# Where the split second weights and the split hidden values of a two-layer expert kernel lie in on-chip memory

## The chip, the cores and the metric

One core of a Trainium2 chip. The metric is the device time of one execution in microseconds (us); the lower, the better.

## The reference

A transform, then two mixture-of-experts layers on the same 24,576 tokens of 256 numbers:

```python
X = np.fft.fft(x, axis=1); X = np.fft.fft(X, axis=2); x = X.real      # 8 x 3072 x 256
# each layer (the first normalises its router's operands and divides by tau):
expert_idx = np.argmax(logits, axis=1); gate_w = softmax(logits)[expert_idx]
for e in range(8):
    h = np.maximum(x[mask] @ w1[e], 0.0)                             # 256 -> 1024
    out[mask] = gate_w[mask, None] * (h @ w2[e])                     # 1024 -> 256
```

The inputs and outputs are float32. The second layer takes the output of the first as its input, and routes anew.

## The kernel before

The transform is done by matmuls with tables of cosines and sines. Its tokens are scattered by indirect DMAs into a table in device memory that is sorted by expert. After that the work runs in blocks ("slots") of one expert each: in layer one 41 blocks of 512 tokens and 17 half blocks of 256, in layer two the same again. Four more half blocks of each layer stand in conditionals and are not executed with these inputs. A block loads its rows, and its expert's weights if the expert has changed, then does two products.

Every operand of these products is split into a high and a low part (`float32r`, 4 bytes a number), and each product is done as three matmuls: high by high, low by high, high by low.

- First product, `mm1` (line 1169): per block 48 matmuls (lines 1183 to 1185) of 512 columns (a half block: 48 of 256). The first weights w1h and w1l are the stationary operand, the tokens xh and xl (tile `a`) the moving one. `evac_h` (line 1187) turns the result into the tiles hh (by ACT, with relu) and hl (by the vector engine, DVE): eight rows, f = 0 to 7, of 512 numbers per partition.
- Second product, `mm2` (line 1196): for each of the four groups of 128 tokens (two in a half block), and for each f, three matmuls: hh by w2h (line 1202), hl by w2h (1203), hh by w2l (1204). Here hh and hl are the stationary operand, 128 columns at a time, and row f of w2h or w2l is the moving one. In layer two a row has 256 numbers. In layer one it has 264: eight columns more give the next layer's router logits.
- `split2` (line 1123) makes w2h (ACT) and w2l (DVE) for the next block while a block computes. Both tiles have two buffers, used in turn; hh and hl have one each.

The order of all this is written out by a planner (class `Plan`) with due times; the second weights' split falls beside the products of the block before. In the built program the engines' queues hold it in that order.

Where a tile's rows lie is set by hand. Lines 1127 to 1130 give the row width w, the offset o of w2h in its tile, and the further offset z of w2l, all in numbers of 4 bytes; lines 1172 to 1175 give the width of the rows of hh and hl and their offset, 16. Before, a row of layer one is as wide as its data, 264, and begins at 32 + 264 f (w2h) or 40 + 264 f (w2l), so its address is a multiple of 64 bytes or 32 bytes past one in turn; hh and hl have rows of 520. In layer two rows are 256 wide from offset 0, and those of hh and hl 512 wide from offset 16. In the built program the tiles' own starts are multiples of 64 bytes, and modulo 256 bytes they are all the same.

The identity matrix `ident` (line 240) is made by two POOL instructions (`make_identity`, line 243) and read by the transposes of `gate_columns` (line 980) during the transform.

Of the kernel before, what the change touches and what calls it, by code (L numbers as in the profile page):

```python
# [10 lines left out]
F32 = mybir.dt.float32  # L11
F32R = mybir.dt.float32r
# [207 lines left out]
def build(tc, x, x0, prep, ctab, ctab8, t2, t2t, misc, embt, tau, w1a, w2a, w2t, wg2, w1b, w2b, out):  # L220
    nc = tc.nc
# [4 lines left out]
    with ExitStack() as top:  # L226
        cp = top.enter_context(tc.tile_pool(name="const", bufs=1))
# [6 lines left out]
            name=nc.get_next_instruction_name(), act_func_set_id=EXP_LN_SET, ins=[], outs=[], engine=A.engine))  # L234
# [2 lines left out]

        mt = cp.tile([128, _o], F32, name="mt")
        mc = {k: mt[:, a:b] for k, (a, b) in MISC.items()}
        ident = cp.tile([128, 128], F32, name="ident")  # L240
        ones = cp.tile([128, 128], BF16, name="ones")
        V.memset(ones, 1.0)
        make_identity(nc, ident)
        tri = cp.tile([128, 128], BF16, name="tri")
        carry = [cp.tile([128, 8], F32, name=f"carry{i}") for i in range(2)]
        rw1 = cp.tile([128, 2, F], F32, name="rw1")
# [255 lines left out]
        fp = fx.enter_context(tc.tile_pool(name="fft", bufs=1))  # L502
# [9 lines left out]
        tb1 = fp.tile([128, 1], F32, name="tau1")  # L512
        wg = fp.tile([128, 2, 32], F32, name="wg")
        V.memset(wg, 0.0)
        onef = fp.tile([128, 128], F32, name="onef")
        V.memset(onef, 1.0)
        tiny = fo.tile([128, 1], F32, name="tiny", bufs=1)
# [538 lines left out]
        slots = []  # L1056
# [9 lines left out]
        pools = {}  # L1066
# [56 lines left out]
        def split2(i, q):  # L1123
            st = S_[i]
            raw = st["raw"]
            if "w2h" not in st:
                w, o, z = (264, 32, 8) if slots[i][0] == 0 else (256, 0, 0)
                for n, k in (("w2h", o), ("w2l", o + z)):
                    t = pools["sb"].tile([128, 8 * 264 + 64], F32R, name=n)
                    st[n] = t[:, k : k + 8 * w].rearrange("p (a b) -> p a b", a=8)  # L1130
            fs = slice(2 * q, 2 * q + 2)
            pairs = [(raw[1][:, fs], fs, slice(0, 256))]
            if slots[i][0] == 0 and q == 0:
                pairs.append((raw[2].rearrange("p (a b) -> p a b", b=8), slice(0, 8), slice(256, 264)))
            for src, f, cs in pairs:
                hi = st["w2h"][:, f, cs]
                act(hi, src, AF.Copy)
                tt(V, st["w2l"][:, f, cs], src, hi.bitcast(F32), ALU.subtract)
# [30 lines left out]
        def mm1(i, k):  # L1169
            st, n, nf = S_[i], 128 * slots[i][3], 4 // slots[i][3]  # L1170
            if k == 0:
                w = 520 if slots[i][0] == 0 else 512
                for e, gap in (("hh", 128), ("hl", 80)):
                    t = pools["sb"].tile([128, 8 * 512 + gap], F32R, name=e, bufs=1)
                    st[e] = t[:, 16 : 16 + 8 * w].rearrange("p (a b) -> p a b", a=8)
            ps = st["ph", k] = pools["h"].tile([128, 512], F32, name="ph")
            for g in range(nf):
                f = nf * k + g
                fs = slice(f * 128, f * 128 + 128)
                o = ps[:, g * n : g * n + n]  # L1180
                for c in range(2):
                    a, z = (g == 0 and c == 0), (g == nf - 1 and c == 1)
                    P.matmul(o, st["w1h"][:, c, fs], st["xh"][:, c, :n], start=a, stop=False)  # L1183
                    P.matmul(o, st["w1h"][:, c, fs], st["xl"][:, c, :n], start=False, stop=False)  # L1184
                    P.matmul(o, st["w1l"][:, c, fs], st["xh"][:, c, :n], start=False, stop=z)  # L1185
# [64 lines left out]
        def stages(plan, i, t):  # L1250

            layer, key, j, ns = slots[i]
            a, tB = dA[i], t[1]
            for k in range(2 * ns):
                plan.add(t[0] + a * k / (2 * ns), lambda i=i, k=k: mm1(i, k))
                plan.add(t[0] + a * (k + 1) / (2 * ns) + 0.1, lambda i=i, k=k: evac_h(i, k))
            for q in range(ns):
                plan.add(tB + 2.75 * q, lambda i=i, q=q: mm2(i, q))
                plan.add(tB + 2.75 * (q + 1) + 0.1, lambda i=i, q=q: evac_y(i, q))
            te = tB + 2.75 * ns + 0.5  # L1260
            plan.add(tB + 0.2, lambda i=i: ids(i))
            if layer == 0:
                st = S_[i]
                route(plan, te, ns, lambda st=st, ns=ns: st["gt"][:, :ns],
                      lambda st=st, ns=ns: [(st["y"][:, :ns, 256:257], 0, ns)], 1, lambda q, st=st: st["y"][:, q, 0:W],
                      lambda: qr.tile([128, 512], F32, name="pr"), dt=0.3, rank=3.6 if i in (0, 1, 4, 5) else 1.8,
                      pen=(lambda st=st: st["pen"]) if ns == 2 else None)
                plan.add(te + 2.5, lambda i=i: put_ids(i))
                plan.add(te + 1.3, lambda i=i: split_y(i))
            else:  # L1270
                for q in range(ns):
                    plan.add(te + 0.1 * q, lambda i=i, q=q: store(i, q))
            return te
# [4 lines left out]
        def rest(layer):  # L1278
# [4 lines left out]
            def block(j):  # L1283
                i = n_ + layer * (NS - NSF) + j - NSF
                if not own:
                    R = [fo.tile([128, 8, W], F32, name="R", bufs=6).rearrange("p a b -> p (a b)") for _ in range(3)]
                    own["x"] = pools["sb"].tile([128, 4, 256], F32, name="xk", bufs=1).rearrange("p a b -> p (a b)")[:, 0 : 2 * W].rearrange("p (a b) -> p a b", a=2)
                    for k, n in enumerate(("xh", "xl")):
                        o = 2 * W + k * 512
                        own[n] = R[0][:, o : o + 512].bitcast(F32R).rearrange("p (a b) -> p a b", a=2)  # L1290
                    own["raw"] = (
                        R[1][:, 0 : 2 * F].rearrange("p (a b) -> p a b", a=2),
                        R[2][:, 0 : 8 * D].rearrange("p (a b) -> p a b", a=8),
                        R[0][:, 2 * W + 1024 : 2 * W + 1088],
                    )
                S_[i].update(own)
                p = Plan()
                p.add(0.0, lambda: load_rows(i))
                p.add(0.1, lambda: load_w(i, 0))
                p.add(0.2, lambda: load_w(i, 1))  # L1300
                p.add(2.1, lambda: join(i, 0))
                p.add(2.2, lambda: evac_x(i, 0, 0))
                p.add(2.3, lambda: evac_x(i, 0, 1))
                for q in range(4):
                    p.add(3.0 + q, lambda q=q: split1(i, q))
                for q in range(4):
                    p.add(7.0 + q, lambda q=q: split2(i, q))
                stages(p, i, (7.0, 13.0))
                p.run()
                own.update({k: S_[i][k] for k in ("w1h", "w1l", "w2h", "w2l")})  # L1310
# [14 lines left out]
        for i in range(n_):  # L1325
            layer, key, j, ns = slots[i]
            t, a = sA[i], dA[i]
# [7 lines left out]
            for q in range(4):  # L1335
                if q < 2 and i and ns == 4:
                    plan.add(sA[i - 1] + dA[i - 1] + dT[i] + (0.7 + 0.18 * q) * dB[i - 1], lambda i=i, q=q: split2(i, q))
                elif ns == 4:
                    plan.add(t + a * (0.3 + 0.25 * (q - 2)) + 0.3, lambda i=i, q=q: split2(i, q))
                else:  # L1340
                    plan.add(t + a * (-0.08 + 0.21 * q) + 0.3, lambda i=i, q=q: split2(i, q))
# [21 lines left out]
        for k, (b, j) in enumerate([(b, j) for b in range(EARLY, B) for j in (2, 0, 1)]):  # L1363
            t, dt = (sA[1] + 14.0 + 26.0 * k, 2.7) if b <= KNOWN[1] else (sA[n1 + (k - 6) * 2] + 1.0, 5.0)
# [55 lines left out]
```

## Time and profile before

| | us |
|---|---|
| median of 3 runs | 2522.08 (2516.24 to 2531.93) |
| profiled execution, its own time | 2522.99 |
| its span, first to last instruction | 2521.2 |
| TensorE busy | 2464.8 |
| DVE, ACT, POOL busy | 1718.6, 1546.5, 644.0 |

The span is what the trace shows; the 1.8 us around it are not in it. Matmuls overlap each other, so that TensorE's busy time says that it has work, not how fast it goes: for that one takes from the timeline when matmuls start. PE is TensorE's matmuls, PEld its weight loads. Lines are those of the listing.

### The profile page before, as it was taken

To read this page: it belongs to the slowest core of one execution; us is meant where nothing else is said; L and a number is where in the kernel's file an instruction comes from. 1 tells how busy PE (TensorE), PEld (TensorE's weight loads), DVE (VectorE), ACT (ScalarE), POOL (GpSimd) and SP (SyncE) were. 2 spreads that over 40 slices of the span, in tenths; PEclk is the share of its full clock that TensorE was granted. 3 is DMA by queue.
4 is the path that set the end of the run, shared out by engine and by line. 5 is a ranking of instruction groups with operands and counts; after the bars stand their busy time and mean duration, and the time that the engine had idled before them with its cause. 6 is when DMAs were issued, how large, how long until landed. Compare 5 with 4: busy or idle time off the path is not lost. (4 is left out here: it accounts for less than half of the span.)

```text
span 2521.2 us, 47343 instructions
## 1 busy us (share of the span) xinstructions
PE 2464.8 (98%) x16634; PEld 2233.7 (89%) x16634; DVE 1718.6 (68%) x3760; ACT 1546.5 (61%) x3311; POOL 644.0 (26%) x603
## 2 busy tenths in 40 slices
PE   7989999999999999999999999999999999999998
PEld 5767898889988998899898989899999999999998
DVE  7785877766676666666888766555555666555876
ACT  4756676666666666665776655555555555555775
POOL 0486245234342111112111211111111111111111
PEclk9999999999999999999999999999999999999999
DMA  8597555444543354433344322421221344313631
GB/s 302 196 305 226 146 148 152 126 110 135 140 115 81 102 139 117 125 97 73 106 139 106 93 67 66 114 84 44 83 51 49 89 143 116 116 47 128 198 98 33
DMA packets 336054, 302.84 MB, mean 120 GB/s; under 512 B 277454, under 2 KB 294277, under 8 KB 321469
## 3 DMA queue, kind: packets, MB, share of 16 engines
q1 hardware_dynamic: 306600, 223.39, 32.7%
q0 software_dynamic: 28528, 76.20, 9.2%
q8 instruction: 135, 2.21, 0.4%
q14 instruction: 114, 0.93, 0.1%
q10 hardware_dynamic: 677, 0.11, 0.0%
HBM read 292.93 MB, written 91.62 MB: 153 GB/s over the span
## 5 line engine op out<-in xcount | busy, mean ns | idle before, releaser
L1203 PE MATMUL p<-w2h,hl 128*128 128x264 f32 (+1 forms) x3168 | 895.3, 283 | 12.5 <-DVE hl L1193 12.2
L1204 PE MATMUL p<-w2l,hh 128*128 128x264 f32 (+1 forms) x3168 | 890.7, 281 | 0.0
L1202 PE MATMUL p<-w2h,hh 128*128 128x264 f32 (+1 forms) x3168 | 885.7, 280 | 1.1 <-ACT gt L224 1.1
L1193 DVE SCALAR_TENSOR_TENSOR hl<-ph,hh 128x512 fp32r<-128x512 f32 x792 | 544.2, 688 | 285.9 <-ACT hh L224 278.2
L224 ACT ACTIVATE hh<-ph 128x512 fp32r<-128x512 f32 x792 | 470.6, 597 | 362.9 <-PE ph L1185 362.3
L1183 PE MATMUL ph<-a,w1h 128*128 128x512 f32 (+1 forms) x1856 | 669.7, 361 | 4.7 <-DVEq L1312 2.0
L1185 PE MATMUL ph<-a,w1l 128*128 128x512 f32 (+1 forms) x1856 | 666.6, 359 | 0.0
L1184 PE MATMUL ph<-a,w1h 128*128 128x512 f32 (+1 forms) x1856 | 665.9, 359 | 0.4 <-DVE a L223 0.4
L1203 PEld LDWEIGHTS p<-w2h,hl 128*128 128x128 f32 x3168 | 594.7, 188 | 24.7 <-DVE hl L1193 19.3
L1202 PEld LDWEIGHTS p<-w2h,hh 128*128 128x128 f32 x3168 | 596.4, 188 | 5.0 <-ACT gt L224 1.5
L1204 PEld LDWEIGHTS p<-w2l,hh 128*128 128x128 f32 x3168 | 598.2, 189 | 0.0
L223 DVE TENSOR_TENSOR w2l<-rw,w2h 128x512 fp32r<-128x512 f32 x464 | 318.9, 687 | 250.3 <-ACT w2h L224 246.2
L1243 POOL DMA_INDIRECT out<-yo,oix x198 | 194.7, 983 | 890.9 <-ACT yo L224 854.3
L330 POOL DMA_INDIRECT xs<-yo,ix x198 | 214.3, 1082 | 757.9 <-ACT hh L224 489.3
L1183 PEld LDWEIGHTS ph<-a,w1h 128*128 128x128 f32 x1856 | 349.2, 188 | 55.0 <-ACT w2h L224 2.1
L1185 PEld LDWEIGHTS ph<-a,w1l 128*128 128x128 f32 x1856 | 349.3, 188 | 53.6
L1184 PEld LDWEIGHTS ph<-a,w1h 128*128 128x128 f32 x1856 | 349.2, 188 | 50.2 <-DVE a L223 0.7
L223 DVE TENSOR_TENSOR w1l<-rw,w1h 128x512 fp32r<-128x512 f32 x464 | 307.9, 687 | 93.9 <-ACT w1h L224 93.1
L224 ACT ACTIVATE w2h<-rw 128x512 fp32r<-128x512 f32 x464 | 290.7, 627 | 23.0 <-DMA rw<-in_w2b 12.1
L224 ACT ACTIVATE w1h<-rw 128x512 fp32r<-128x512 f32 x464 | 275.2, 626 | 4.0 <-DMA rw<-in_w1a 4.0
L224 ACT ACTIVATE yo<-p,R 128x256 f32<-128x256 f32 x198 | 94.3, 476 | 218.0 <-PE p L1204 216.5
L224 ACT ACTIVATE R<-p,R 128x256 f32<-128x256 f32 x198 | 93.7, 473 | 201.4 <-PE p L1204 201.3
(217 smaller groups left out, 1969.6 us busy)
## 6 DMA issues: line engine op xcount, KB each, us to landing
rw<-in_w1a SPq DMA_DIRECT2D x58, 1024.0 KB
rw<-in_w2a SPq DMA_DIRECT2D x58, 1024.0 KB
rw<-in_w1b SPq DMA_DIRECT2D x58, 1024.0 KB
rw<-in_w2b SPq DMA_DIRECT2D x58, 1024.0 KB
X<-in_x SPq DMA_DIRECT2D x48, 512.0 KB
rw<-in_w2t SPq DMA_DIRECT2D x8, 1024.0 KB
kept<-Rk SPq DMA_DIRECT2D x15, 512.0 KB
xk<-kept SPq DMA_DIRECT2D x12, 512.0 KB
```

The source lines that it names most:

```text
L223: tt = lambda eng, o, a, b, op: eng.tensor_tensor(out=o, in0=a, in1=b, op=op)
L224: act = lambda o, i, f, **k: A.activation(out=o, in_=i, func=f, **k)
L330: table.scattered(G.indirect_dma_start(out=table.buf, out_offset=bass.IndirectOffsetOnAxis(ap=st["ix"][:, j : j + 1], axis=0), in_=rows(j) ...
L1183: P.matmul(o, st["w1h"][:, c, fs], st["xh"][:, c, :n], start=a, stop=False)
L1184: P.matmul(o, st["w1h"][:, c, fs], st["xl"][:, c, :n], start=False, stop=False)
L1185: P.matmul(o, st["w1l"][:, c, fs], st["xh"][:, c, :n], start=False, stop=z)
L1193: V.scalar_tensor_tensor(out=st["hl"][:, fs, :n], in0=ps, scalar=0.0, in1=hi.bitcast(F32), op0=ALU.max, op1=ALU.subtract)
L1202: P.matmul(ps[:, :n], st["hh"][:, f, js], st["w2h"][:, f, :n], start=(f == 0), stop=False)
L1203: P.matmul(ps[:, :n], st["hl"][:, f, js], st["w2h"][:, f, :n], start=False, stop=False)
L1204: P.matmul(ps[:, :n], st["hh"][:, f, js], st["w2l"][:, f, :n], start=False, stop=(f == 7))
L1243: ins = G.indirect_dma_start(out=out, out_offset=bass.IndirectOffsetOnAxis(ap=st["ix"][:, j : j + 1], axis=0), in_=st["y"][:, j, 0:256], i ...
```

## The change

- Layer one: rows of w2h and w2l are 272 numbers (1088 bytes) apart instead of 264. The offset of w2h is 0, 16, 32 or 48 numbers, by the slot's number modulo four; w2l lies 16 further. The columns that are written and multiplied stay 264.
- hh and hl: offset 0 instead of 16; in layer one rows of 528 instead of 520. In layer two they stay 512.
- Layer two: the offset of w2h and w2l is 48 instead of 0.
- The tiles grow by 64 numbers (w2h, w2l) and 48 (hl). To make room, `ident` moves from the pool that lasts through the whole kernel to the one of the transform, whose memory the block tiles take later; with it `make_identity` is recorded one memset of the vector engine later.

The matmuls, their number, shapes and order are the same; every engine's instructions stand in the same order as before. ACT, DVE, SP and POOL each get one wait more, for POOL's two instructions on `ident`, in front of their first use of the memory that `ident` shares.

```diff
-        ident = cp.tile([128, 128], F32, name="ident")
         ones = cp.tile([128, 128], BF16, name="ones")
         V.memset(ones, 1.0)
-        make_identity(nc, ident)
...
         wg = fp.tile([128, 2, 32], F32, name="wg")
         V.memset(wg, 0.0)
+        ident = fp.tile([128, 128], F32, name="ident")
+        make_identity(nc, ident)
...
             if "w2h" not in st:
-                w, o, z = (264, 32, 8) if slots[i][0] == 0 else (256, 0, 0)
+                w, o, z = (272, 16 * (i % 4), 16) if slots[i][0] == 0 else (256, 48, 0)
                 for n, k in (("w2h", o), ("w2l", o + z)):
-                    t = pools["sb"].tile([128, 8 * 264 + 64], F32R, name=n)
+                    t = pools["sb"].tile([128, 8 * 272 + 64], F32R, name=n)
                     st[n] = t[:, k : k + 8 * w].rearrange("p (a b) -> p a b", a=8)
...
             if k == 0:
-                w = 520 if slots[i][0] == 0 else 512
-                for e, gap in (("hh", 128), ("hl", 80)):
-                    t = pools["sb"].tile([128, 8 * 512 + gap], F32R, name=e, bufs=1)
-                    st[e] = t[:, 16 : 16 + 8 * w].rearrange("p (a b) -> p a b", a=8)
+                w = 528 if slots[i][0] == 0 else 512
+                for e in ("hh", "hl"):
+                    t = pools["sb"].tile([128, 8 * 528], F32R, name=e, bufs=1)
+                    st[e] = t[:, 0 : 8 * w].rearrange("p (a b) -> p a b", a=8)
```

## Rows read from the trace of the kernel before

**Rows 1.** The page: span, busy times, and the granted clock in 40 slices.

```profile
PE 2464.8 (98%) x16634; PEld 2233.7 (89%) x16634; DVE 1718.6 (68%) x3760; ACT 1546.5 (61%) x3311; POOL 644.0 (26%) x603
...
PEclk9999999999999999999999999999999999999999
```

**Rows 2.** Waits of TensorE: us in total, times, longest us.

```profile
PE p L1203 <- DVE hl L1193: 12.2, 24, 1.3
```

**Rows 3.** Stretches (us; busy us of each engine, instructions; clock; DMA) by stage.

```profile
251.50:1420.30 1168.80, 1154.02 (x7953) 1053.39 (x7953) 836.38 (x2211) 770.49 (x1562) 320.88 (x293) 1.00 0.46 120
1420.30:2521.20 1100.90, 1091.76 (x7542) 1009.68 (x7540) 697.10 (x1180) 623.14 (x1156) 197.68 (x201) 1.00 0.31 89
```

**Rows 4.** Groups by line and shape (busy us, mean ns, idle): the hh*w2h products.

```profile
L1202 PE MATMUL p<-w2h,hh 128*128 128x264 f32 x1584 | 446.3, 282 | 1.1 <-ACT gt L224 1.1
L1202 PE MATMUL p<-w2h,hh 128*128 128x256 f32 x1584 | 439.4, 277 | 0.0
```

**Rows 5.** Timeline of TensorE (start us, length us): second products of one layer-one block.

```profile
590.98 0.28 PE L1202 MATMUL p<-w2h,hh 128*128 128x264 f32 x1
...
602.53 0.39 PE L1183 MATMUL ph<-a,w1h 128*128 128x512 f32 x1
```

**Rows 6.** Timeline: a layer-two block's second products, its successor's first, and second again.

```profile
1940.52 0.28 PE L1202 MATMUL p<-w2h,hh 128*128 128x256 f32 x1
...
1951.42 0.39 PE L1183 MATMUL ph<-a,w1h 128*128 128x512 f32 x1
...
1962.41 0.28 PE L1202 MATMUL p<-w2h,hh 128*128 128x256 f32 x1
```

**Rows 7.** Timeline: second products of layer one's first block.

```profile
263.96 0.29 PE L1203 MATMUL p<-w2h,hl 128*128 128x264 f32 x1
...
275.60 0.39 PE L1183 MATMUL ph<-a,w1h 128*128 128x512 f32 x1
```

**Rows 8.** Timeline: second products of a slower layer-two block.

```profile
1566.64 0.28 PE L1202 MATMUL p<-w2h,hh 128*128 128x256 f32 x1
...
1577.94 0.40 PE L1183 MATMUL ph<-a,w1h 128*128 128x512 f32 x1
```

**Rows 9.** Timeline: a layer-two half block, 48 first products and then 48 second.

```profile
2323.61 0.28 PE L1183 MATMUL ph<-a,w1h 128*128 128x256 f32 x1
...
2329.05 0.28 PE L1202 MATMUL p<-w2h,hh 128*128 128x256 f32 x1
...
2334.71 0.28 PE L1183 MATMUL ph<-a,w1h 128*128 128x256 f32 x1
```

**Rows 10.** Timeline of POOL: the last instruction on the identity.

```profile
1.04 0.29 POOL masks.py:199 TENSOR_SCALAR_AFFINE_SELECT ident<-ident 128x128 f32<-128x128 f32 x1
```

**Rows 11.** Line 980, the identity's readers: durations min/median/max, first and last start.

```profile
L980 PE MATMUL px<-ident,gs x16: 271/272/273, 54.1 to 217.3; 128*128 128x128 f32 x16
```

**Rows 12.** Groups: ACT's writes of w2h in layer one, then in layer two.

```profile
L224 ACT ACTIVATE w2h<-rw 128x512 fp32r<-128x512 f32 x233 | 146.4, 629 | 12.2 <-DMA rw<-in_w2a 10.8 <-DMA rw<-in_w2b 1.4
...
L224 ACT ACTIVATE w2h<-rw 128x512 fp32r<-128x512 f32 x232 | 144.9, 625 | 12.2 <-DMA rw<-in_w2b 12.1
```

**Rows 13.** Timeline of TensorE: the products of two successive rows in layer one.

```profile
600.01 0.28 PE L1202 MATMUL p<-w2h,hh 128*128 128x264 f32 x1
600.12 0.28 PE L1203 MATMUL p<-w2h,hl 128*128 128x264 f32 x1
600.24 0.28 PE L1204 MATMUL p<-w2l,hh 128*128 128x264 f32 x1
600.37 0.28 PE L1202 MATMUL p<-w2h,hh 128*128 128x264 f32 x1
600.48 0.28 PE L1203 MATMUL p<-w2h,hl 128*128 128x264 f32 x1
600.60 0.28 PE L1204 MATMUL p<-w2l,hh 128*128 128x264 f32 x1
```

**Rows 14.** Timeline of the weight loads: the one beside the first of these.

```profile
600.01 0.19 PEld L1203 LDWEIGHTS p<-w2h,hl 128*128 128x128 f32 x1
```

## The prediction

> **What bounds the kernel now.** I read the page first. TensorE is busy for 2464.8 of 2521.2 us and its granted clock is at the top digit in all 40 slices [rows 1], so this is one long stream of matmuls at 2.4 GHz, the upper level, and a change counts only as far as it changes how fast that stream runs or how often it stops. The waits of TensorE say how often it stops: the largest is 12.2 us over the whole run, L1203 (second half of a product) waiting for the tile hl [rows 2]. The stretches then say where the time lies: layer one takes 1168.8 us from 251.5 on, layer two 1100.9 [rows 3]. The two layers have the same number of matmuls with the second weights, 3 x 1584 each (one of the three products stands in the rows), 264 columns wide in layer one and 256 wide in layer two [rows 4]. These 4752 matmuls of layer one (41 blocks of 96, 17 half blocks of 48) are what the change re-addresses.
>
> A busy time cannot price them, because each matmul lasts about 280 ns while the next starts about 120 ns later. So I take start to start, from the timeline. In a layer-one block the 96 matmuls run from 590.98 to 602.53 us: 11.55 / 96 = 120.3 ns each [rows 5]. In a layer-two block they run from 1940.52 to 1951.42: 10.90 / 96 = 113.5 ns, and the 48 matmuls of 512 columns behind them take 10.99 us, 228.9 ns each [rows 6]. Between these two sizes a column costs (228.9 - 113.5) / 256 = 0.45 ns, so 264 columns at layer two's rate would cost 113.5 + 8 x 0.45 = 117.1 ns. Layer one pays 120.3: 3.2 ns per matmul, 15 us in all, are over and above its eight extra columns. That is the most that a better address could give back if it only brought layer one to layer two's rate.
>
> But the same form also runs slower at the same addresses. The first two blocks of layer one take (275.60 - 263.96) / 95 = 122.5 ns [rows 7]; in layer two there is a row of six blocks at (1577.94 - 1566.64) / 96 = 117.7 ns [rows 8], and its half blocks change between 113.3 and 117.9 within one block [rows 9]. A block's tiles lie in one of two fixed buffers, and both buffers occur with either rate, so the rate is a pattern that the stream falls into and keeps until a stall breaks it, not a function of the address alone. The spread of the three runs (2516 to 2532 us) is of the size that such patterns make.
>
> **The change part by part.**
> *Order and waits.* The program's instructions stand in the same order on every engine. One wait is added on each of ACT, DVE, SP and POOL: the identity's new place will later be overwritten by the block tiles, so those wait for POOL's two instructions on it, the second of which ends at 1.33 us [rows 10], some 250 us before the tiles are first written. Behind the waiting instructions the blocks' first loads are queued, and they find the wait long over. Cost 0; if it were not covered, it would delay the first block by what POOL is late, and POOL has nothing else to do then.
> *Identity moved.* The same two POOL instructions are recorded after a memset of the vector engine instead of before it, and stand at the same place of POOL's own queue; the first reader runs at 54.1 us [rows 11]. Cost 0, hidden by those 52 us.
> *Writers of the tiles.* ACT writes w2h in 629 ns in layer one (rows 264 apart) and 625 ns in layer two (rows 256 apart) [rows 12]. A row step of 272 is priced by that difference, 4 ns either way, 233 x 4 = 0.9 us on an engine that is busy for 770 of layer one's 1168.8 us [rows 3]; the vector engine behind it is busy for 836. Both have the cover of the matmuls, and without it 0.9 us would be the price. I take 0.
> *The reads.* What is left is which bytes TensorE reads together. While one matmul streams a row of w2h or w2l, the weights of the next one (a row of hh or hl) are loaded: their load starts within 0.01 us of that matmul [rows 13, 14]. In bytes, modulo 256 (the span of the four places; all tile starts agree modulo that in both programs), the weights lie 64 behind the streamed row in layer one before, for all three products and all eight rows, and 64 ahead in layer two. So the distance was already steady; what is new is that rows no longer start alternately on a multiple of 64 and 32 past one, and that layer one's distance is 0, 64, 128, 192 behind in turn. 192 behind is 64 ahead, so layer two stays as it was, and one place in four of layer one gets layer two's distance.
> Does the start on 64 matter? Inside a block the steps are 0.11, 0.12, 0.13 us for the three products of one row and 0.11, 0.12 again for the next, though one of the two starts on 64 and the other 32 past it [rows 13]. So I price the alignment itself at 0. Its bounds are 0 and the 3.2 ns from above.
> The four places: the one with layer two's distance I take at layer two's rate, 117.1 ns. It holds 10 blocks and 4 half blocks, 10 x 96 + 4 x 48 = 1152 matmuls x -3.2 ns = -3.7 us. The one with the old distance stays at 120.3. The two that no row shows lie between 117.1 and 122.5 ns (layer two's rate, and the worst that rows give for this width), 2400 matmuls, so -7.7 to +5.3 us; I take 120.3, the rate nearest to what 264 columns do nearly always (58 of the 60 runs of products in layer one). In half blocks 0.6 us of the gain could vanish into the wait for hl.
> Sum: 0 + 0 + 0 - 3.7 = -3.7 us on the profiled execution's 2523.0 us (span 2521.2 and 1.8 around it): 2519. The median of the runs is 2522.1, 0.9 us below the profiled one, which is less than this sum can tell.
>
> The Trainium skill speaks against a gain. Its page "SBUF — State Buffer", section "Specifications (TRN2)", gives SBUF 16-byte lines; every row of either kernel starts on a multiple of 16, so by it the step to 64 buys nothing, as rows 13 also suggest. The same page, section "SBUF: two separate sides", says that TensorE's port never waits for another engine, and its part "A bandwidth-pool intuition that's wrong (but worth ruling out)" gives the weight load a read port of its own; by that no distance matters and the time would stay at 2523. The trace neither confirms nor denies it: two rates at one distance need some other cause.
>
> **The rivals.**
> *Nothing moves.* Columns and the phase in which a run starts set the pattern, the place doesn't. For it: two rates at the same addresses [rows 7 to 9], no difference between even and odd rows [rows 13]. Against it: layer one keeps 120.3 through stalls that let layer two change, as if something fixed held it. Time 2523.
> *All of layer one at 117.1.* The row that ends in half of a 64-byte piece and the next that starts in one is what holds layer one at 120.3, and the alignment frees it at every distance. For it: layer two, all rows on 64, reaches 113.5. Against it: the even and odd rows. 4752 x -3.2 = -15.2: 2508.
> *Layer one falls into the 122.5 pattern* (slower). Distances 0 or 128 make streamed row and loaded weights meet more often, and since a pattern persists, the blocks of the other places inherit it. It decides once two or more places in four run at 122.5. For it: the pattern exists in the first two blocks. Against it: it never came back in 58 runs of products. All of layer one: 4752 x 2.2 = +10.5: 2533.5.
> *Layer two falls into 117.7* (slower). A block then pays 96 x (117.7 - 113.5) = 0.40 us more [rows 6, 8]. The stall at which the pattern is drawn anew comes at another moment, and the 35 blocks that now run fast run slow: 35 x 0.40 = 14, and 1.8 for the eight half blocks' products that are fast now: 2539. For it: six blocks in a row did so. Against it: it lasted only until the next stall.
>
> **How the numbers follow.** One place in four gains: 0.36, 2519. Nothing moves: 0.26, 2523. All of layer one gains: 0.17, 2508. Layer one slower: 0.12, 2533.5. Layer two slower: 0.09, 2539. Runs of this kernel differ by some 0.3% from their median, and 1%, 25 us, is about what a measurement can tell from no change. No single case reaches 25 us; faster by that needs a rate below any seen at this width, slower by that needs both slow cases together. So faster 0.04, same 0.91, slower 0.05. The range runs from the good case less some spread, 2503, to the worst single case, 2539. The likeliest case's own range, with its unknown places, is 2511 to 2525.
>
> **What would show it.** Right: the same wait rows; layer-one blocks with indices 3, 7, 11 at about 117 ns per second-layer matmul and 11.24 us per 96, the others at 11.55, repeating every four blocks; layer-two rates of 113.5 and 117.7 as before. Wrong: no difference with the index modulo four (places don't matter, or the alignment does it all, by the level), a rate below 117 in all layer-one blocks, products in layer one at 122 or more, a changed 228.9 ns of the 512-wide matmuls, whose tiles keep their places, or a new wait of TensorE.

## The result and the profile after

| | before | after |
|---|---|---|
| median of 4 runs each, us | 2520.27 (2516.24 to 2531.93) | 2541.68 (2538.96 to 2542.07) |
| profiled execution, us | 2522.99 | 2542.07 |
| its span, us | 2521.2 | 2540.3 |

The changed kernel is 0.84% slower: ratio 1.0084, 95% interval 1.0056 to 1.0112. That is inside the 1% that the prediction called no change, and outside its range of 2503 to 2539. Two of its rivals, layer one slower and layer two slower, came together.

The page after, to be laid beside [rows 1]:

```profile
PE 2488.9 (98%) x16634; PEld 2256.8 (89%) x16634; DVE 1717.1 (68%) x3760; ACT 1546.3 (61%) x3311; POOL 642.1 (25%) x603
...
PEclk9999999999999999999999999999999999999999
```

TensorE has as many instructions as before and 24.1 us more busy time, at the same granted clock; the other engines have what they had. The largest wait of TensorE, beside [rows 2] (us in total, times, longest):

```profile
PE p L1203 <- DVE hl L1193: 11.1, 23, 1.4
```

So no wait was added: the stream itself runs slower. The stretches by stage, beside [rows 3], cut at the first L1183 of layer two (us; busy us of PE, PEld, DVE, ACT, POOL; clock; DMA):

```profile
251.50:1422.77 1171.27, 1158.37 (x7957) 1057.29 (x7958) 836.47 (x2212) 772.29 (x1566) 320.80 (x294) 1.00 0.46 120
1422.77:2540.30 1117.53, 1109.16 (x7542) 1026.86 (x7540) 696.61 (x1180) 622.46 (x1156) 195.72 (x201) 1.00 0.31 88
```

The first stretch takes 2.5 us more (1168.8 before), layer two 16.6 us more (1100.9 before): 19.1 us, which is the difference of the two spans. Of the 2.5, 1.4 lie ahead of the blocks: the first L1183 starts at 253.0 us (durations, then first and last start in the row below) and in the trace of before at 251.6. Layer one itself is 1.1 us longer. Nearly all of the loss is in the layer of which the prediction said that it stays as it was.

```profile
L1183 PE MATMUL ph<-a,w1h x1856: 276/394/503, 253.0 to 2529.3; 128*128 128x512 f32 x132, 128*128 128x256 f32 x54
```

The timeline of four successive layer-one blocks (start us, length us): the first second product of each, and the first L1183 behind it.

```profile
456.32 0.28 PE L1202 MATMUL p<-w2h,hh 128*128 128x264 f32 x1
...
467.90 0.39 PE L1183 MATMUL ph<-a,w1h 128*128 128x512 f32 x1
...
479.15 0.28 PE L1202 MATMUL p<-w2h,hh 128*128 128x264 f32 x1
...
490.83 0.40 PE L1183 MATMUL ph<-a,w1h 128*128 128x512 f32 x1
...
502.10 0.28 PE L1202 MATMUL p<-w2h,hh 128*128 128x264 f32 x1
...
513.80 0.39 PE L1183 MATMUL ph<-a,w1h 128*128 128x512 f32 x1
...
525.06 0.28 PE L1202 MATMUL p<-w2h,hh 128*128 128x264 f32 x1
...
536.77 0.40 PE L1183 MATMUL ph<-a,w1h 128*128 128x512 f32 x1
```

11.58, 11.68, 11.70 and 11.71 us per 96 matmuls: 120.6, 121.7, 121.9 and 122.0 ns each, where [rows 5] have 120.3. These are blocks with index modulo four 0, 1, 2, 3, and the pattern repeats every four blocks through the 41 big blocks of layer one (the products of the half blocks behind them are broken by stops). Not one place gains. Below, means over a block's single steps are given, by the trace's nanoseconds: 120.6, 121.6, 121.8, 122.0.

Layer two, a block and the start of the next block's second products; then a half block:

```profile
1614.27 0.28 PE L1202 MATMUL p<-w2h,hh 128*128 128x256 f32 x1
...
1625.57 0.40 PE L1183 MATMUL ph<-a,w1h 128*128 128x512 f32 x1
...
1636.58 0.28 PE L1202 MATMUL p<-w2h,hh 128*128 128x256 f32 x1
...
2345.04 0.28 PE L1202 MATMUL p<-w2h,hh 128*128 128x256 f32 x1
...
2350.69 0.28 PE L1183 MATMUL ph<-a,w1h 128*128 128x256 f32 x1
```

11.30 us per 96 (117.7 ns) and 5.65 per 48 (117.7 ns). All 41 blocks and all 17 half blocks of layer two run so; before, 35 blocks and eight half blocks ran at 113.5 [rows 6, 8, 9]. The first products behind the block take 11.01 us, 229 ns each, as before. Summed over the traces' starts (steps without a stop): the second products of layer two take 117.74 ns on average against 114.49, times 4749 = +15.4 us; the half blocks' first products +1.8, the 512-wide ones +0.5; stops -1.1. In layer one the second products take 121.50 ns against 120.46, times 4752 = +4.9 us; the first products +0.8; the stops of the stream come to 30.7 us instead of 35.3, -4.6. That last term is partly chance: in the run e8 below, whose layer one is that of before, the stops come to 32.7, and in e9, whose layer one is the changed one, to 31.2.

ACT's writes of w2h take 626 ns on average in the row below (629 and 625 in [rows 12]), and POOL's last instruction on the identity still starts at 1.0 us, its first reader at 55.0. Those parts cost nothing.

```profile
L224 ACT ACTIVATE w2h<-rw 128x512 fp32r<-128x512 f32 x464 | 290.4, 626 | 18.6 <-DMA rw<-in_w2b 9.9
```

### The profile page after: what moved, and what is told of

It is laid out like the page before. It is cut to its first block, busy times and chain, and to the rows that moved or that the text cites. A ratio compares the mean times of both kernels' runs of the same rounds, so it can differ in the third digit from the quotient of the medians.

```text
span 2540.3 us, 47343 instructions
## 1 busy us (share of the span) xinstructions
PE 2488.9 (98%) x16634; PEld 2256.8 (89%) x16634; DVE 1717.1 (68%) x3760; ACT 1546.3 (61%) x3311; POOL 642.1 (25%) x603
## 5 line engine op out<-in xcount | busy, mean ns | idle before, releaser
L1203 PE MATMUL p<-w2h,hl 128*128 128x264 f32 (+1 forms) x3168 | 901.8, 285 | 11.4 <-DVE hl L1193 11.1
L1202 PE MATMUL p<-w2h,hh 128*128 128x264 f32 (+1 forms) x3168 | 896.3, 283 | 0.5 <-ACT gt L224 0.5
L1204 PE MATMUL p<-w2l,hh 128*128 128x264 f32 (+1 forms) x3168 | 893.6, 282 | 0.0
L1183 PE MATMUL ph<-a,w1h 128*128 128x512 f32 (+1 forms) x1856 | 673.9, 363 | 3.9 <-DVEq L1312 2.0
L1185 PE MATMUL ph<-a,w1l 128*128 128x512 f32 (+1 forms) x1856 | 667.0, 359 | 0.0
L1184 PE MATMUL ph<-a,w1h 128*128 128x512 f32 (+1 forms) x1856 | 664.0, 358 | 0.4 <-DVE a L223 0.4
L1203 PEld LDWEIGHTS p<-w2h,hl 128*128 128x128 f32 x3168 | 594.6, 188 | 23.1 <-DVE hl L1193 18.1
L1204 PEld LDWEIGHTS p<-w2l,hh 128*128 128x128 f32 x3168 | 602.6, 190 | 0.0
L1202 PEld LDWEIGHTS p<-w2h,hh 128*128 128x128 f32 x3168 | 595.8, 188 | 4.0 <-ACT gt L224 0.9
L1185 PEld LDWEIGHTS ph<-a,w1l 128*128 128x128 f32 x1856 | 349.2, 188 | 57.6
L1183 PEld LDWEIGHTS ph<-a,w1h 128*128 128x128 f32 x1856 | 349.5, 188 | 51.1 <-ACT w2h L224 2.1
L1184 PEld LDWEIGHTS ph<-a,w1h 128*128 128x128 f32 x1856 | 349.1, 188 | 50.5 <-DVE a L223 0.7
```

The source lines that it names most:

```text
L1202: P.matmul(ps[:, :n], st["hh"][:, f, js], st["w2h"][:, f, :n], start=(f == 0), stop=False)
L1203: P.matmul(ps[:, :n], st["hl"][:, f, js], st["w2h"][:, f, :n], start=False, stop=False)
L1204: P.matmul(ps[:, :n], st["hh"][:, f, js], st["w2l"][:, f, :n], start=False, stop=(f == 7))
```

## The experiments

Two theories went into the runs. *P*: the place (start of the streamed rows w2, start of the weights hh) sets the rate. *K*: a pattern is drawn at a start or a stop of the stream and then kept, at any place. Places are given as offsets in numbers (w2, hh). "Distance" is the weights' start against the streamed row's, in bytes modulo 256. The first six experiments ran on other chips: e1 to e4 on one where the kernel before took 2588 us (median of 17 runs) instead of 2520, e5 and e6 on one where it took 2607 (one run). The granted clock of all six falls below the top digit in some early slices of the page, in the transform and in some of them in early layer one; so rates of blocks are compared, more than totals. e3 to e7 are one run each.

### Undoing one layer at a time

**e1**, the changed kernel with layer two's old place:

```diff
-                w, o, z = (272, 16 * (i % 4), 16) if slots[i][0] == 0 else (256, 48, 0)
+                w, o, z = (272, 16 * (i % 4), 16) if slots[i][0] == 0 else (256, 0, 0)
...
-                w = 528 if slots[i][0] == 0 else 512
+                w, p = (528, 0) if slots[i][0] == 0 else (512, 16)
...
-                    st[e] = t[:, 0 : 8 * w].rearrange("p (a b) -> p a b", a=8)
+                    st[e] = t[:, p : p + 8 * w].rearrange("p (a b) -> p a b", a=8)
```

> The changed kernel with layer two's offsets as before the change (w2h and w2l at 0, hh and hl at 16); layer one as changed. Theory P (place: where the tiles lie decides a block's rate): layer two's products return from 117.7 to 113.5 ns, layer one keeps 120.6 to 122.0, time about 2541.7 - 17 = 2525 us. Theory K (the pattern is drawn when the stream begins or stalls, and kept; the place only shifts the draw): the entry from layer one is that of the changed kernel, so layer two may stay at 117.7 in all or most blocks, up to 2541 us.

Measured: ratio to before 1.0048 (1.0019 to 1.0078). Layer one 120.6, 121.6, 121.8, 122.0 as in the changed kernel. Layer two at its old place: two blocks at 113.5, then a stop of the stream (a first-product step of 305 ns), and from there 39 blocks at 117.8. The old place can be slow for a whole layer, so the place alone does not decide there.

**e2**, the changed kernel with layer one's old place:

```diff
-                w, o, z = (272, 16 * (i % 4), 16) if slots[i][0] == 0 else (256, 48, 0)
+                w, o, z = (264, 32, 8) if slots[i][0] == 0 else (256, 48, 0)
...
-                w = 528 if slots[i][0] == 0 else 512
+                w, p = (520, 16) if slots[i][0] == 0 else (512, 0)
...
-                    st[e] = t[:, 0 : 8 * w].rearrange("p (a b) -> p a b", a=8)
+                    st[e] = t[:, p : p + 8 * w].rearrange("p (a b) -> p a b", a=8)
```

> The changed kernel with layer one's rows and offsets as before the change (264, 520, offsets 32 and 40, hh and hl at 16); layer two as changed. Theory P: layer one's products return to 120.3 ns (4752 x 1.2 ns = 5.7 us less than the changed kernel), layer two stays at 117.7 in all blocks, about 2536 us. Theory K: layer two enters from the old layer one and should be fast in most blocks as before, about 2520 us.

Measured: ratio 1.0058 (1.0022 to 1.0094). Layer one 120.2 to 120.5 in its big blocks but for three, which begin at 122.5 (of these below, with e7); layer two 117.7 to 117.8 in every block and half block. Each layer's loss belongs to its own part of the change. In layer two the new place looks slow always, the old one sometimes.

### Shifting the stream by one matmul

The starts of the first products show where K could live. Their steps come in a turn of three, 226, 229 and 232 ns, one for each of L1183, L1184, L1185. Which product gets which step differs from block to block; I call (226, 229, 232) the first turn, (232, 226, 229) the second, (229, 232, 226) the third. One matmul more ahead of a block shifts the turn by one.

**e3**, the changed kernel with one repeated first product ahead of the fifth, 13th and 21st block of layer two:

```diff
+                    if k == 0 and a and i in (62, 70, 78):
+                        P.matmul(o, st["w1h"][:, c, fs], st["xh"][:, c, :n], start=True, stop=True)
                     P.matmul(o, st["w1h"][:, c, fs], st["xh"][:, c, :n], start=a, stop=False)
```

> The changed kernel with one matmul of layer two's first product done twice in the 5th, 13th and 21st block of layer two, which shifts the sequence of three by one each time; the output is the same, the work is 0.7 us more. Theory P: every block of layer two stays at 117.7 ns, 2542 us. Theory K: at one or two of the three nudges the blocks after it change to 113.5 ns and stay so; if from the 5th block on, 2526 us.

Measured: 2599.2 us, on the chip where the kernel before takes 2588. The turn shifted in the nudged blocks, into the one that is fast at the old place, but every block stayed at 117.7 and the next was back in the second turn. At the new place a fast turn of the old one does not help.

**e6**, the kernel before with the same nudge in layer-two blocks 6, 12, 18 (one) and 24, 30 (two), counted from 0:

```diff
+                    for _ in range({64: 1, 70: 1, 76: 1, 82: 2, 88: 2}.get(i, 0) if k == 0 and a else 0):
+                        P.matmul(o, st["w1h"][:, c, fs], st["xh"][:, c, :n], start=True, stop=True)
                     P.matmul(o, st["w1h"][:, c, fs], st["xh"][:, c, :n], start=a, stop=False)
```

> The kernel before, with one extra first-product matmul (a repetition whose result is overwritten) in layer-two blocks 6, 12 and 18, and two in blocks 24 and 30, which shifts the turn of three in which the first products' steps come (226, 229, 232 ns). The kernel costs 7 x 0.23 us = 1.6 us more by itself. Theory K (the turn at the entry decides at this place, and is kept): the rate of layer two's blocks changes at the nudged blocks and stays until the next nudge or stall: from 113.4 to about 117.8 ns a product, or back, at least at one of the five; a block that is slow then costs 0.42 us more. Theory P (the place alone decides): the rate does not change at any nudge, and at the place of before all blocks between two stalls run alike, 113.4 or 117.8, as without the nudges.

Measured (the timeline; L1204 is this kernel's first second product, L1184 the extra matmul, L1185 the next block's first product): the block ahead of the first nudge and the nudged one, then the block ahead of the third nudge and the nudged one.

```profile
1615.09 0.28 PE L1204 MATMUL p<-w2h,hh 128*128 128x256 f32 x1
...
1626.00 0.39 PE L1184 MATMUL ph<-a,w1h 128*128 128x512 f32 x1
...
1637.21 0.28 PE L1204 MATMUL p<-w2h,hh 128*128 128x256 f32 x1
...
1648.52 0.40 PE L1185 MATMUL ph<-a,w1h 128*128 128x512 f32 x1
...
1881.78 0.28 PE L1204 MATMUL p<-w2h,hh 128*128 128x256 f32 x1
...
1893.09 0.40 PE L1184 MATMUL ph<-a,w1h 128*128 128x512 f32 x1
...
1904.33 0.28 PE L1204 MATMUL p<-w2h,hh 128*128 128x256 f32 x1
...
1915.22 0.39 PE L1185 MATMUL ph<-a,w1h 128*128 128x512 f32 x1
```

10.91 us, then with one more matmul ahead of it 11.31; later 11.31, then 10.89. The same instructions at the same addresses run at 113.6 or 117.8 ns by how many matmuls came before. Behind the first nudge the slow pattern lasted two blocks, until a stop ended it; behind the second it kept for six, until the third nudge ended it. The two double nudges left the rate fast, since two of the three turns are fast here. At the old place K's main point holds (the pattern decides and is kept), and P falls.

### Scanning places

**e4** put eight layouts into each layer, five blocks each, to tell alignment, distance and absolute place apart.

```diff
-                w, o, z = (272, 16 * (i % 4), 16) if slots[i][0] == 0 else (256, 48, 0)
+                w, o, z = lay(slots, i)[:3]
...
-                    t = pools["sb"].tile([128, 8 * 528], F32R, name=e, bufs=1)
-                    st[e] = t[:, 0 : 8 * w].rearrange("p (a b) -> p a b", a=8)
+                    t = pools["sb"].tile([128, 8 * 528 + 16], F32R, name=e, bufs=1)
+                    st[e] = t[:, p : p + 8 * w].rearrange("p (a b) -> p a b", a=8)
```

> The changed kernel with eight layouts per layer, five blocks each. Layer one, as row width and offset of w2h, further offset of w2l, row width and offset of hh: 264,32,8,520,16 (before); 272,32,16,528,16 (the same distance, all on 64 bytes); then 264 with offsets 16, 48 and 0; then 264,32,8,528,16 and 272,32,16,520,16 (distance not steady); 264,32,16,520,16. Layer two, all rows 256 and 512, as offsets of w2h, w2l and hh: 0,0,16 (before); 16,16,32; 32,32,48; 48,48,0 (changed), all at one distance; then hh at 0 and w2 at 0, 16, 32; then 0,16,16. Theory P: each layout has a rate of its own from its first or second block on: 120.3 for the old one in layer one, 121 to 122 for the one on 64 bytes; 113.5 for the old one in layer two, 117.7 for the changed one. Theory K: the rate of a block follows that of the block before, whatever the layout, and changes after stalls.

Measured: in layer one, where no stop broke the block, 120.35 for the old rows and 120.55 for rows on multiples of 64 at the old distance; 120.3 to 123.4 for the rest. In layer two all four layouts at the old distance 118.2 to 118.3, even the kernel before's own. The run is spoiled in part by its edit: the tiles of hh are 64 bytes longer, so hl lies 64 bytes elsewhere against hh (in the built program hh, w2h and w2l start alike modulo 256, as in the other kernels, and hl 64 further). That by itself took layer two's fast rate away: the place of hl counts too.

**e5** is the same scan with the right tile lengths, and sixteen layouts (two blocks each) in layer two.

```diff
+ONE = [(264, 32, 8, 520, 16), (272, 16, 16, 528, 0), (264, 16, 8, 520, 0), (272, 0, 16, 528, 0),
+       (264, 0, 8, 520, 0), (272, 48, 16, 528, 0), (264, 48, 8, 520, 32), (264, 32, 8, 520, 0)]
+TWO = [(256, o, 0, 512, h) for h in (16, 0, 32, 48) for o in (0, 16, 32, 48)]
...
+                    st[e] = t[:, p : p + 8 * w].rearrange("p (a b) -> p a b", a=8)
```

> The changed kernel's tiles, but other places: in layer one eight layouts, five blocks each; in layer two sixteen layouts, two blocks each (start of hh and hl at 16, 0, 32, 48 numbers, for each of them start of w2h and w2l at 0, 16, 32, 48), the rest of layer two at the place of before (w2 0, hh 16). The tiles of hh and hl start as in the changed kernel, so their distance is the right one this time. Theory P (the place decides the rate): in layer two some of the sixteen layouts run at 113.3 to 113.6 ns a product and others at 117.7 and above, and the two known ones come out as known: start 16 with w2 0 can be 113.3, start 0 with w2 48 is 117.7. If only the distance between the two counts, the four layouts with the same difference read alike; if the absolute place counts too, they do not. In layer one the aligned rows at the old distance (272, 16, 16, 528, 0) read 120.6, not less than the old rows' 120.3. Theory K (a pattern drawn at a start or stall and kept): layouts that follow each other without a stall have the rate of the one ahead of them, 113.3 or 117.7, whatever their place, and the rate changes only behind a first product step of over 300 ns. Mixed: some places only slow (117.7 and above), the others either.

Measured, from the starts of the trace, ns a product:

```
layer one                       distance        264 rows     272 rows (all on 64)
w2 32 hh 16                     64 behind       120.3
w2 16 hh 0                      64 behind       120.4        121.6-121.7
w2 48 hh 32                     64 behind       120.3
w2 0  hh 0                      none            121.4        120.6
w2 48 hh 0                      64 ahead                     122.0
w2 32 hh 0                      128             122.4
layer two: no distance 119.8 to 120.0 in all 8 blocks; 128: 118.6 to 118.8 in 6 and 120.0 in 2;
           64 ahead or behind: 113.3 to 113.6 in 7 of 16 blocks, 117.7 to 117.9 in 9
```

The rates of layer one are those of blocks without a stop. A place has its rate there, the same to 0.1 ns as in the changed kernel (120.6, 121.6, 122.0). Rows on 64 at the old distance are 1.3 ns slower than rows of 264 at the same start (w2 16, hh 0), but at no distance (w2 0, hh 0) they are 0.8 ns faster: by itself the alignment is neither a gain nor without effect. In layer two, 113.3 to 113.6 appears only at a distance of 64, on either side, and there in some blocks only.

**e7** took the eight places at that distance and shifted the turn in each by single nudges, five blocks a place.

```diff
+TWO = [(256, o, 0, 512, h) for o, h in ((48, 0), (0, 16), (16, 32), (32, 48), (16, 0), (32, 16), (48, 32), (0, 48))]
...
+                    for _ in range(1 if k == 0 and a and (i in (24, 28, 32, 36) or 58 <= i < 98 and (i - 58) % 5) else 0):
+                        P.matmul(o, st["w1h"][:, c, fs], st["xh"][:, c, :n], start=True, stop=True)
```

> Every block of layer two but the last and the half blocks gets one of eight places (five blocks each), those whose streamed row and loaded weights stand 64 bytes apart modulo 256: four with the weights ahead (among them that of the kernel before and that of the changed kernel), four with the weights behind. In each five, blocks two to five begin with one extra first-product matmul, so that the turn of three is another at each and all three come. Half blocks take the eight places two by two, without extra matmuls. Layer one lies as before, with an extra matmul in blocks 24, 28, 32 and 36. Theory K (the turn at the entry decides, at any place of this distance): each place shows 113.4 ns in some of its five blocks and 117.8 in others, the changed kernel's place (w2 48, hh 0) too. Theory P (the place decides): the changed kernel's place reads 117.7 in all five, and at least one other place reads one rate in all five. Mixed (place and turn both): the changed kernel's place is 117.7 in all five, the place of before is slow in one turn of three and fast in two. In layer one both expect 120.3 ns in all blocks, since there no stall has changed the rate; a rate of 117.1 behind one of its four extra matmuls would show that the turn rules there too.

Measured, on a chip at the speed of the first: layer one 120.3 in all four nudged blocks. But there the nudge did not reach the second products. Among the first products of a big block, mostly after 18 of the 48, layer one has six small matmuls of the next layer's routing (below with the first product ahead of them and the one behind):

```profile
811.15 0.40 PE L1195 MATMUL ph<-a,w1l 128*128 128x512 f32 x1
811.39 0.19 PE L295 MATMUL pr<-o,ones 128*128 128x32 bf16 x1
...
811.48 0.22 PE L300 MATMUL pr<-o,ones 128*128 128x24 bf16 x3
811.56 0.48 PE L1193 MATMUL ph<-a,w1h 128*128 128x512 f32 x1
```

Ahead of them the nudged blocks step by 232, 226, 229 and their neighbours by 229, 232, 226; behind them both step by 232, 226, 229, the second turn, and so enter the second products alike. Where a block of layer one did enter otherwise, the turn told. The second and third block of the kernel before, same form and same place, entered with the third turn and with the second (the first L1202 and the L1183 behind, twice):

```profile
288.21 0.28 PE L1202 MATMUL p<-w2h,hh 128*128 128x264 f32 x1
...
299.97 0.39 PE L1183 MATMUL ph<-a,w1h 128*128 128x512 f32 x1
...
312.58 0.28 PE L1202 MATMUL p<-w2h,hh 128*128 128x264 f32 x1
...
324.13 0.39 PE L1183 MATMUL ph<-a,w1h 128*128 128x512 f32 x1
```

11.76 and 11.55 us, 122.5 and 120.3 ns. In the traces of before, e2, e6, e7 and e8, whose layer one lies at the old place, 192 of 200 big blocks (all but each run's first) enter with the second turn, and up to their first stop they run at 120.2 to 120.6. The other eight enter with the third, and all eight begin at 122.5; two keep it to the end, in the others it ends at a stop or at a single odd step. So the turn tells in layer one too; it just hardly ever varies there. These blocks entered so of themselves: no run set the turn at the entry in layer one.

In layer two, the changed kernel's place was slow in all its five blocks; but it came once more, in the last big block, behind a place that had left the first products at 233 ns each instead of in a turn. L1212 is this kernel's first second product; the two blocks are one of the five, and that last one:

```profile
1496.54 0.28 PE L1212 MATMUL p<-w2h,hh 128*128 128x256 f32 x1
...
1507.85 0.40 PE L1192 MATMUL ph<-a,w1h 128*128 128x512 f32 x1
...
2326.25 0.28 PE L1212 MATMUL p<-w2h,hh 128*128 128x256 f32 x1
...
2337.14 0.28 PE L1193 MATMUL ph<-a,w1h 128*128 128x256 f32 x1
```

11.31 and 10.89 us at one place. So "always slow" is not right either: the new place is slow in each of the three turns, and fast in the one block entered without a turn. Sorting all big blocks of layer two of before, after and every run but e4 by place and turn at entry leaves no place and turn with two rates (beyond 0.5 ns). Three places (ns a product, turn of the next block, number of blocks):

```
place               first turn            second turn           third turn
w2 0  hh 16 before  113.5 -> first  (72)  113.5 -> first  (12)  117.8 -> third  (55)
w2 48 hh 0  after   117.8 -> second  (9)  117.8 -> second (119) 117.8 -> second  (2)
w2 48 hh 32         117.8 -> second  (4)  113.5 -> second  (1)  117.8 -> second  (2)
```

(The counts of the last row are those ahead of the next two runs. "Next" holds where no stop or nudge comes between.) Place and turn together set the rate and the next turn. The old place has a fast trap (first) and a slow one (third); the new one has a slow trap only. The third row is another case: every turn leads to its one fast turn.

### A place that frees itself

**e8** is the kernel before with that third place for layer two's big blocks, **e9** the changed kernel with it (hh at 32 instead of 0; half blocks as before).

```diff
-                w, o, z = (264, 32, 8) if slots[i][0] == 0 else (256, 0, 0)
+                w, o, z = (264, 32, 8) if slots[i][0] == 0 else (256, 48 if slots[i][3] == 4 else 0, 0)
...
-                w = 520 if slots[i][0] == 0 else 512
+                w, p = (520, 16) if slots[i][0] == 0 else (512, 32 if slots[i][3] == 4 else 16)
...
-                    st[e] = t[:, 16 : 16 + 8 * w].rearrange("p (a b) -> p a b", a=8)
+                    st[e] = t[:, p : p + 8 * w].rearrange("p (a b) -> p a b", a=8)
```

> The kernel before, with layer two's big blocks at another place: w2h and w2l start at 48 numbers, hh and hl at 32 (weights 64 bytes behind the streamed row). Layer one and the half blocks of layer two lie as before. In the two scans this place ran at 117.8 ns when entered with the first of the three turns (steps 226, 229, 232 at the three products) or the third (229, 232, 226), at 113.3 with the second (232, 226, 229), and each time the next first products came in the second turn. Theory place-and-turn (each place maps a turn to a rate and to the next turn): behind each stall at most one block runs at 117.8, all others at 113.5; no row of six slow blocks. Against the kernel before that is between 0 and 35 x 0.4 = 14 us faster, by how many slow blocks that one draws in its runs (six, 2.5 us, in its profile): ratio 0.995 to 1.000. Theory K alone (a pattern drawn at a stall and kept, the same lottery at any place): rows of slow blocks as before, about a third of the draws, ratio 1.000. Theory P alone (one rate for a place): all big blocks at 117.8 or all at 113.5.

> The changed kernel, with hh and hl of layer two's big blocks at 32 numbers instead of 0 (w2h and w2l stay at 48), and the half blocks of layer two at the place of before. Layer one stays as changed. Theory place-and-turn: big blocks of layer two at 113.5 ns but for one or two behind a stall, half blocks 113.3 and 117.8 in turn as before; what is left against the kernel before is layer one's 5.7 us (4752 products at 1.2 ns), less what that one loses in slow blocks: ratio 1.000 to 1.003, where the changed kernel had 1.008. Theory P with the distance alone (64 behind is slow, as in layer one): 117.8 in layer two, ratio 1.008 as the changed kernel. Theory K alone: slow in rows, as in the run that put layer two back, ratio 1.002 to 1.008.

Measured in e8: of 41 blocks one is at 117.8, behind a stop, as in e9. The timeline: the block ahead, the stop (in brackets the idle time of TensorE and what ended it), the block behind it, and the next.

```profile
1583.06 0.28 PE L1202 MATMUL p<-w2h,hh 128*128 128x256 f32 x1
...
1593.94 0.40 PE L1183 MATMUL ph<-a,w1h 128*128 128x512 f32 x1
...
1601.83 0.50 PE L1183 MATMUL ph<-a,w1h 128*128 128x512 f32 x1 [0.85 <-DVE hl L1193]
...
1606.07 0.28 PE L1202 MATMUL p<-w2h,hh 128*128 128x256 f32 x1
...
1617.37 0.40 PE L1183 MATMUL ph<-a,w1h 128*128 128x512 f32 x1
...
1628.38 0.28 PE L1202 MATMUL p<-w2h,hh 128*128 128x256 f32 x1
...
1639.26 0.40 PE L1183 MATMUL ph<-a,w1h 128*128 128x512 f32 x1
```

10.88 us, 11.30 behind the stop (entered with the first turn), then 10.88 again: the block after a disturbance pays 0.42 us and the stream is back. Both theories alone had expected otherwise.

Times, with the kernel before on the same chip at 2518.63 us (median of 23 runs): e8 2516.07 (12 runs), ratio 0.9987 (0.9972 to 1.0003), not told apart from before; e9 2520.45 (10 runs), ratio 0.9994 (0.9973 to 1.0016). (The ratios are estimates over all runs and differ a little from the quotients of the medians, 1.0007 for e9.) Another start of hh in layer two's big blocks, with its half blocks put back, takes the changed kernel's 1.0084 away; its layer one is unmended (120.6 to 122.0). What that costs is seen best between e8 and e9, whose layer two lies alike (they differ in layer one and in the identity's place): layer one takes 1165.6 us in the trace of e8 and 1170.3 in that of e9, and the medians are 4.4 us apart. What e8 changes is the spread. The 23 runs of before lie between 2513.0 and 2521.0 (16 of them) or between 2528.7 and 2533.0 (seven), with none between; the twelve of e8 lie between 2513.7 and 2521.8. A gap of some 14 us is what 33 blocks times 0.42 us come to, the blocks behind the last stop when it leaves the third turn. That fits; those seven runs have no trace, so it is not shown.

## Why the prediction was wrong

By its own steps:

- *What bounds the kernel, waits, identity, writers*: right. No new wait, L1203's wait 11.1 us against 12.2, ACT's writes 626 ns.
- *Layer two, "192 behind is 64 ahead, so layer two stays as it was"*: the step that failed, priced 0 and measured +16.6 us. It took the distance modulo 256 for all that counts of a place. The distance is the same, and the absolute start, together with the turn in which the stream enters, decides the rate: the old place is fast in two of three turns, the new one in none (e3, e6, e7). The part ahead of it had said that the rate is not a function of the address alone; it did not ask the counterpart, what an address does to the pattern.
- *Layer one, the place with layer two's distance, "at layer two's rate, 117.1 ns"*: wrong, 122.0, the slowest of the four. A rate of 256 columns was carried over to 264 ones by the distance alone. At 264 columns each place has rates of its own (e1, e2, e5), and none of those tried came near 117.1; the lowest is 120.3.
- *"The one with the old distance stays at 120.3"*: 121.6. *"So I price the alignment itself at 0"*: e5 shows +1.3 ns for rows of 272 at this place (w2 16, hh 0), and -0.8 at w2 0, hh 0. The bounds (0 and the 3.2 ns to be gained) lacked the side on which it fell. The two unseen places came within their bounds, 120.6 and 121.8 against 117.1 to 122.5. Sum of the rates: +4.9 us where -3.7 was forecast; in this pair of runs shorter stops took back nearly as much, and the blocks began 1.4 us later.
- *The rivals*: "layer two falls into 117.7" gave 15.8 us, and 16.6 were measured; its mechanism, a moment that is drawn otherwise, was wrong, since at the new place each of the three turns loses, so the near hit is luck. What spoke against it, that it "lasted only until the next stall", holds for the old place alone. "Layer one falls into the 122.5 pattern" was right that the places are slower, and too large (10.5 against 4.9); the pattern itself, 122.5 at the old place, is what the third turn gives there, and the blocks did not fall into it: each place went to a rate of its own. The two were treated as exclusive; they have separate causes, and both occurred.

The pages cited ahead are answered too. The Trainium skill, "SBUF — State Buffer", part "A bandwidth-pool intuition that's wrong (but worth ruling out)", gives the weight load a read port of its own, by which no distance would matter. The scans disagree with what the prediction drew from it: at 256 columns a block takes 119.8 to 120.0 ns where streamed row and weights start alike modulo 256, whatever the turn, and 113.3 to 117.9 where they start 64 apart (e5). What the prediction took from the Trainium skill's 16-byte lines (same page), that the step to 64 buys nothing, holds for the change as a whole; by itself the step is not without effect (e5: +1.3 ns at one place, -0.8 at another).

## What to carry to other kernels

When matmuls follow each other without waits, the start-to-start step is the quantity to read, block by block, and a program that re-addresses an operand has to be checked in every stage whose addresses it touches, also the one that is "only kept in step". A rate that comes in two levels at the same addresses is a state, not noise: find what carries it across blocks (here the turn of the steps ahead), and choose a place from which every state leads back to the fast one, rather than one that is fast in the profile at hand. A nudge that tests for such a state has to be followed to where it is to act: in layer one of e7 it was lost on the way. A time in two clusters with a gap is a hint of such a state.

## What the runs showed of the hardware that was not expected

- One matmul more, 0.23 us, ahead of a block changes the rate of its 96 second products from 113.6 to 117.8 ns and that of the five blocks behind it (e6).
- First products of 512 columns step by 226, 229, 232 ns in a turn; behind some places they step by 233 or 234 each (e7, blocks at w2 0, hh 48).
- At a distance of 0 between streamed row and weights, 256 columns take 119.8 to 120.0 ns in all eight blocks, in every turn, against 113.3 at best (e5): 6%, by address alone.
- At 264 columns in rows of 264 the turn counts too: 120.3 ns entered with the second, 122.5 with the third (before, e2, e6, e7, e8). Six small matmuls among the first products, 0.3 us, undo the shift of a nudge ahead of them (e7).

What stays open is what in TensorE or its reads makes the turn and ties it to the place; the runs only show that the pair of them decides.
